# One matmul on block-diagonal operands, or two column tiles of 64: the sums and weighted sums of a windowed attention

## The chip, the cores and the metric

The kernel runs on one core of a Trainium2 chip. The metric is device time in microseconds (us) of that core, lower is better. TensorE (PE) does the matmuls, with a row of its own for loads of the stationary operand (PEld); VectorE (DVE), ScalarE (ACT) and GpSimd (POOL) do the elementwise work; SyncE (SP) issues most of the DMAs.

## The reference

Inputs are q, k and v of shape 8 x 8 x 576 x 64 (batch, heads, sequence, head dimension) and two weight matrices, 512 x 2048 and 2048 x 512.

```
scores = (q @ k.T) / sqrt(64)              # per batch and head, 576 x 576
scores = where(|i - j| <= 32, scores, -1e9)
attn   = exp(scores - max); attn = attn / (sum(attn) + 1e-9)
x      = attn @ v                          # 4608 tokens x 512 once the heads are joined
h      = x @ w_in; g = max(0.01 * h, h)
out    = g @ w_out                         # 4608 x 512, float32
```

The kernel needs no maximum, and it divides after the product with v: x = (sum of e * v) / (sum of e), with e the masked exponentials. So it has, per head, one sum of e over the keys and one weighted sum of v.

## The kernel before

**Tiling of the attention.** Two heads make a pair, four pairs a batch. One *step* is one pair and one half of the sequence (288 queries), so there are 64 steps: 8 batches x 2 halves x 4 pairs. The keys are cut into blocks of 64. The partitions of a step's tiles hold 64 keys of the first head (0 to 63) and 64 of the second (64 to 127).

The stationary operands are block-diagonal, 128 x 128: `kbd` holds a block of the transposed keys of the two heads, `vbd` a block of their values, and `ones_bd` two 64 x 64 blocks of ones; the other two quarters are zero. With such an operand one matmul works for both heads, and its output has the first head in partitions 0 to 63 and the second in 64 to 127.

**A step** has these parts:

- `score` (L275): five matmuls of `kbd` blocks with q into the PSUM tile `ps`, each for the 32 to 64 queries that see this block (in two interleaved columns, so 64 to 128 moving columns); then the exponential on ScalarE (L280) and the mask on GpSimd (L282), which gives `prob`. Blocks with even and odd numbers lie in two layers n of `prob`, so that every query has a place in each.
- `join` (L292, from step 12 on): VectorE adds the two layers into `both`.
- `sums` (L301, or L304 for the first 12 steps): one matmul of `ones_bd` with `both`, 288 moving columns, or two matmuls that accumulate over the two layers. The result `s` is inverted on VectorE (L309) into `r`.
- `product` (L320): five matmuls of `vbd` blocks with `prob`, with 64, 128, 96, 128 and 128 moving columns, together 544, that accumulate into `x`.
- `scaled` (L334): VectorE multiplies `x` by `r` into the ring `xT`, which the MLP reads.

**The MLP.** For each group of 288 tokens 16 tiles of h (L348, four matmuls of 288 columns each, 1024 in all) and then, for each 128 tokens, an output tile (L390, 16 matmuls of up to 512 columns, 592 in all). Before these, the activation is on ScalarE (L355).

**Order.** It is written out by hand: the engines get their instructions in the order of the program. The first 12 steps are laid out singly, with `sums` and `product` at separate places in part. From step 12 on, a plan gives every step a due time in PE time of the MLP, some 4 us apart, and `spend` calls `step` between two tiles. On TensorE a step of this stage is: five matmuls of `score` for the step after next, then `sums` (one matmul), then `product` (five matmuls), then the MLP again. Nothing in the plan's prices depends on the steps' own PE time.

**PSUM.** `s` and `x` have a buffer of 288 float32 columns each (one bank); `ps` has two banks and the MLP four.

Of the kernel before, what the change touches and what calls it, by code (L numbers as in the profile page):

```python
# [16 lines left out]
def kernel(  # L17
# [14 lines left out]
    nc = tc.nc  # L32
# [78 lines left out]
    ones_bd = const.tile([128, 128], BF16)  # L111
# [9 lines left out]
    vbd = [const.tile([128, NPAIR, NB, 128], BF16, name=f"vbd{i}") for i in range(2)]  # L121
# [145 lines left out]
    def where(i):  # L267
        return i // 8, (i // 4) % 2, i % 4
# [26 lines left out]
    def sums(i):  # L295

        b, hf, p = where(i)
        pr, both, _ = probs[i]
        s = xps.tile([128, HALF], FP32, name="s")
        if both is not None:  # L300
            nc.tensor.matmul(s, ones_bd, both, start=True, stop=True)  # L301
        else:
            for n in range(2):
                nc.tensor.matmul(  # L304
                    s, ones_bd, pr[:, n].rearrange("p c i -> p (c i)"),
                    start=(n == 0), stop=(n == 1),
                )
        r = recip.tile([128, HALF], FP32, name="r")
        nc.vector.reciprocal(r, s)  # L309
        probs[i][2] = r  # L310

    def product(i):

        b, hf, p = where(i)
        pr = probs[i][0]
        x = xps.tile([128, HALF], FP32, name="x")
        x_v = x.rearrange("p (c i) -> p c i", c=2)
        parts = [(n_, *block) for n_ in range(2) for block in WIN[hf][n_]]
        for n_, blk, i0, n in parts:
            nc.tensor.matmul(  # L320
                x_v[:, :, i0:i0 + n], vbd[b % 2][:, p, blk, :], pr[:, n_, :, i0:i0 + n],
                start=(blk == parts[0][1]), stop=(blk == parts[-1][1]), skip_group_check=True,
            )
        probs[i][1] = x

    def place(i):
# [9 lines left out]
    def weighted(i):  # L336
        if probs[i][2] is None:
            sums(i)
        product(i)
        scaled(i)  # L340
# [127 lines left out]
    cast_qk(0, 2, nc.vector)  # L468
    score(1)
    sums(0)  # L470
    next(first)
    next(first)
    product(0)
    keep_busy(ps, 0, 2)
    place_keys()
    cast_qk(0, 3, nc.scalar)
    load_w_in(0, 512)
    scaled(0)
    sums(1)
    keep_busy(ps, 0, 3)  # L480
    load_w_in(512, 1024)
# [10 lines left out]
    score(3)  # L492
    load_w_out(0)
    product(1)
    scaled(1)
    cast_v(0, 2, on_act=True)
# [150 lines left out]
```

## Time and profile before

| what | value |
|---|---|
| time, median of 2 runs | 319.7 us (319.49 and 319.91) |
| the profiled execution, first to last instruction | 318.5 us |
| PE busy | 303.2 us, 95%, 2449 matmuls |
| PEld busy | 204.3 us, 64%, 2449 loads |
| DVE busy | 218.2 us, 69% |
| POOL busy | 191.6 us, 60% |
| ACT busy | 182.6 us, 57% |
| granted TensorE clock, mean | 1.000 |
| matmuls of `sums` | 52 (L301) and 24 (L304) |
| matmuls of `product` | 320 (L320) |

The profiled execution is known by its span alone; the timed runs have what lies around it too, and their median is 1.2 us above the span. A row of the profile's groups gives the line, engine and operation, the output and the inputs with the tile names, the count, the busy time and the mean duration of one. Matmuls are pipelined: one starts before the one ahead has ended, so the recorded duration of one (286 ns for 288 columns) is longer than the time to the start of the next. Where a stream is dense the price of a matmul is that distance between starts, which the timeline gives. The share of a chain's line is the share of the span in which this line was what the end waited for.

### The profile page before, as it was taken

Reading aid. Unit: us, or ns where it says so; the run is one execution under the profiler, and the core shown is the slowest. Engines: PE = TensorE matmul, PEld = TensorE weight load, DVE = VectorE, ACT = ScalarE, POOL = GpSimd, SP = SyncE. Lnnn points to the kernel's source line nnn. Section 1 sums busy time; section 2 is a strip of 40 time slices with the busy share of each in tenths; the row PEclk is TensorE's granted clock in tenths of the full one; section 3 lists DMA queues with packets and bytes.
Section 4 is the critical chain, followed back from the end, with each engine's and each line's share of the span. In section 5 each row is a group of like instructions: output and inputs, shape, how many; then the busy total and the mean of one; then the engine's idle time right before and its main releaser. Section 6 shows DMA issues by size and latency. Waiting matters only on the chain.

```text
span 318.5 us, 6474 instructions
## 1 busy us (share of the span) xinstructions
PE 303.2 (95%) x2449; PEld 204.3 (64%) x2449; DVE 218.2 (69%) x259; ACT 182.6 (57%) x393; POOL 191.6 (60%) x251
## 2 busy tenths in 40 slices
PE   2679998999999999999999999999999999999996
PEld 1467774585765858576765858576665858576653
DVE  5678955869655997688755997688745988565100
ACT  7577698474652828374652828375552837464531
POOL 7798963974546866686546866586637866330000
PEclk9999999999999999999999999999999999999999
DMA  8999999997999995399735995399733430000101
GB/s 179 211 186 218 267 250 203 250 206 181 216 242 196 231 206 150 82 251 203 155 76 127 238 227 136 75 223 232 162 76 104 109 70 33 35 35 2 66 31 71
DMA packets 108400, 49.46 MB, mean 155 GB/s; under 512 B 68816, under 2 KB 103888, under 8 KB 108368
## 3 DMA queue, kind: packets, MB, share of 16 engines
q1 hardware_dynamic: 104144, 44.84, 66.8%
q0 software_dynamic: 4224, 4.19, 8.0%
q8 instruction: 19, 0.31, 0.4%
q14 instruction: 13, 0.11, 0.1%
HBM read 36.70 MB, written 9.44 MB: 145 GB/s over the span
## 4 chain that ended last, share of the span: by engine, by line
PE 89%; DMA 3%; DVE 2%; SPq 1%; POOL 1%; ACT 1%; issue 1%; DVEq 0%; ACTq 0%
PE mm L348 39%; PE mm L390 38%; PE x L320 5%; PE ps L275 4%; DMA kf<-in_k_dram 3%; PE s L301 2%; DVE r L309 2%; SPq L79 1%; POOL w_in_bf L448 1%; DVE xT L334 1%; PE tp L225 1%; PE s L304 1%; ACT vbd L203 0%; SPq L91 0%; POOL prob L282 0%
## 5 line engine op out<-in xcount | busy, mean ns | idle before, releaser
L309 DVE RECIPROCAL r<-s 128x288 f32<-128x288 f32 x64 | 125.2, 1956 | 56.5 <-PE s L301 53.3
L282 POOL TENSOR_TENSOR prob<-e,mask 128x576 bf16<-128x576 bf16 x64 | 81.5, 1274 | 87.8 <-ACT e L280 41.1
L348 PE MATMUL mm<-xT,w_in_bf 128*128 128x288 bf16 x1024 | 134.0, 286 | 0.3
L390 PE MATMUL mm<-w_out_bf,gT 128*128 128x512 bf16 (+2 forms) x592 | 130.4, 373 | 0.2 <-DMA w_out_bf<-in_moe_w_out_dram 0.2
L355 ACT ACTIVATE gT<-mm 128x288 bf16<-128x288 f32 x256 | 101.4, 412 | 24.8 <-PE mm L348 8.5
L348 PEld LDWEIGHTS <-w_in_bf 128*128 128x128 bf16 x1024 | 98.4, 98 | 24.8 <-issue 0.6
L390 PEld LDWEIGHTS <-gT 128*128 128x128 bf16 x592 | 56.3, 98 | 59.6 <-issue 0.3
L395 ACT ACTIVATE o_sb<-mm 128x512 f32<-128x512 f32 (+2 forms) x37 | 21.7, 586 | 92.0 <-PE mm L390 92.0
L280 ACT ACTIVATE e<-ps 128x576 bf16<-128x576 f32 x64 | 41.4, 648 | 9.4 <-PE ps L275 9.2
L197 POOL CAST kb<-kf 96x384 bf16<-96x384 f32 (+1 forms) x56 | 35.5, 656 | 4.6 <-DMA kf<-in_k_dram 4.6
L205 POOL CAST vbd<-vf 64x576 bf16<-64x576 f32 x50 | 34.5, 689 | 1.8 <-DMA vf<-in_v_dram 0.4
L334 DVE TENSOR_TENSOR xT<-x,r 128x288 bf16<-128x288 f32 x64 | 29.3, 458 | 8.2 <-PE x L320 1.2
L260 DVE COPY kbd<-kT 64x576 bf16<-64x576 bf16 x48 | 32.3, 672 | 0.3
L275 PE MATMUL ps<-qT,kbd 128*128 128x128 bf16 (+2 forms) x320 | 26.5, 215 | 1.8 <-DVE kbd L258 1.2
L275 PEld LDWEIGHTS <-kbd 128*128 128x128 bf16 x320 | 21.0, 100 | 10.6 <-DVE kbd L258 1.5
L320 PE MATMUL x<-prob,vbd 128*128 128x128 bf16 (+2 forms) x320 | 26.0, 213 | 1.3 <-ACT vbd L203 0.7
L197 POOL CAST qb<-qf 96x384 bf16<-96x384 f32 x48 | 24.5, 538 | 0.0
L320 PEld LDWEIGHTS <-vbd 128*128 128x128 bf16 x320 | 20.6, 99 | 3.9 <-ACT vbd L203 1.8
L292 DVE TENSOR_TENSOR both<-prob 128x288 bf16<-128x288 bf16 x52 | 19.7, 380 | 0.9
L301 PE MATMUL s<-both,ones_bd 128*128 128x288 bf16 x52 | 14.9, 286 | 0.0
L258 DVE COPY kbd<-kT 64x576 bf16<-64x576 bf16 x16 | 7.1, 444 | 8.7 <-ACT kT L239 8.6
L225 PE MATMUL tp<-ident,qb 96*128 96x96 bf16 x48 | 4.4, 243 | 6.2 <-DVE qb L197 6.2
(43 smaller groups left out, 86.6 us busy)
## 6 DMA issues: line engine op xcount, KB each, us to landing
qf<-in_q_dram SPq DMA_DIRECT2D x32, 288.0 KB, 4.5
kf<-in_k_dram SPq DMA_DIRECT2D x32, 288.0 KB, 5.0
vf<-in_v_dram SPq DMA_DIRECT2D x64, 144.0 KB, 4.2
out_dram<-o_sb SPq DMA_DIRECT2D x35, 256.0 KB, 3.6
w_in_bf<-in_moe_w_in_dram POOLq DMA_DIRECT2D x4, 512.0 KB, 8.6
w_out_bf<-in_moe_w_out_dram POOLq DMA_DIRECT2D x4, 512.0 KB, 16.8
qT<-qb SPq DMA_TRANSPOSE x24, 4.1
kT<-kb SPq DMA_TRANSPOSE x24, 3.2
```

What stands on the lines that cost most here:

```text
L197: eng.tensor_copy(out=to, in_=tok)
L205: nc.gpsimd.tensor_copy(out=vbd[b % 2][r, p, :, r], in_=vf[b, p][r])
L260: nc.vector.tensor_copy(out=to.rearrange("p n (m c) -> p n c m", c=2), in_=kT[r].rearrange("p (c n m) -> p n c m", c=2, n=NB),)
L275: nc.tensor.matmul(ps_v[:, n_, :, i0:i0 + n], kbd[b % 2][:, p, blk], by_c[:, :, hf * EVEN + i0:hf * EVEN + i0 + n], start=True, stop=True,)
L280: nc.scalar.activation(out=e, in_=ps[:, P0:P0 + 2 * HALF], func=AF.Exp, scale=scale)
L282: nc.gpsimd.tensor_mul(pr.rearrange("p n c i -> p (n c i)"), e, mask[hf].rearrange("p n c i -> p (n c i)"),)
L309: nc.vector.reciprocal(r, s)
L320: nc.tensor.matmul(x_v[:, :, i0:i0 + n], vbd[b % 2][:, p, blk, :], pr[:, n_, :, i0:i0 + n], start=(blk == parts[0][1]), stop=(blk == parts ...
L334: nc.vector.tensor_mul(place(i), x, r)
L348: nc.tensor.matmul(h[:, 0:HALF], w_in_bf[:, c, ts(f, 128)], xT[:, c, ds(g * HALF % RING, HALF)], start=(c == 0), stop=(c == DMC - 1),)
L355: nc.scalar.activation(out=gT[:, f, ds(g * HALF % RING, HALF)].rearrange("p (i c) -> p i c", c=2), in_=h[:, 0:HALF].rearrange("p (c i) -> ...
L390: nc.tensor.matmul(o[:, lo:hi], gT[:, f, ds(128 * j % RING, 128)], w_out_bf[:, f, lo:hi], start=(f == 0), stop=(f == FFC - 1),)
```

## The change

`sums` and `product` call TensorE once for each head of the pair. The stationary operand of a call is a half of the columns of the same tile, 64 of 128, with all 128 partitions (so with the half that is zero); the moving operand is the same as before; the output is the half of the PSUM tile that belongs to this head, partitions 0 to 63 or 64 to 127. Every matmul of these two functions, and its load of the stationary operand, becomes two. The two halves of a pair stand directly behind each other. `score`, the MLP, the tiles, buffers and the order are unchanged.

```diff
@@ sums
         s = xps.tile([128, HALF], FP32, name="s")
-        if both is not None:
-            nc.tensor.matmul(s, ones_bd, both, start=True, stop=True)
-        else:
-            for n in range(2):
+        for n in range(1 if both is not None else 2):
+            cols = both if both is not None else pr[:, n].rearrange("p c i -> p (c i)")
+            for r in (slice(0, 64), slice(64, 128)):
                 nc.tensor.matmul(
-                    s, ones_bd, pr[:, n].rearrange("p c i -> p (c i)"),
-                    start=(n == 0), stop=(n == 1),
+                    s[r], ones_bd[:, r], cols, skip_group_check=True,
+                    start=(n == 0), stop=(both is not None or n == 1),
                 )
@@ product
         for n_, blk, i0, n in parts:
-            nc.tensor.matmul(
-                x_v[:, :, i0:i0 + n], vbd[b % 2][:, p, blk, :], pr[:, n_, :, i0:i0 + n],
-                start=(blk == parts[0][1]), stop=(blk == parts[-1][1]), skip_group_check=True,
-            )
+            for r in (slice(0, 64), slice(64, 128)):
+                nc.tensor.matmul(
+                    x_v[r, :, i0:i0 + n], vbd[b % 2][:, p, blk, r], pr[:, n_, :, i0:i0 + n],
+                    start=(blk == parts[0][1]), stop=(blk == parts[-1][1]), skip_group_check=True,
+                )
```

## The prediction

> **What bounds the kernel now.** I read the page's busy times first, then the chain that ended last, then windows by stage, and last the timeline of TensorE around one step. From the page, the busy times, the slices (PE's busy tenths and granted clock) and the chain:
>
> ```profile
> PE 303.2 (95%) x2449; PEld 204.3 (64%) x2449; DVE 218.2 (69%) x259; ACT 182.6 (57%) x393; POOL 191.6 (60%) x251
> ...
> PE   2679998999999999999999999999999999999996
> ...
> PEclk9999999999999999999999999999999999999999
> ...
> PE 89%; DMA 3%; DVE 2%; SPq 1%; POOL 1%; ACT 1%; issue 1%; DVEq 0%; ACTq 0%
> ```
>
> PE is the bound from the fourth slice on, at the full clock, and the chain is PE for 89% of the span. The windows by stage (span, then PE and PEld busy with counts, the other engines, clock, DMA) say where that is exact:
>
> ```profile
> 0.00:36.00 36.00, 24.96 (x236) 19.22 (x237) 27.34 (x34) 25.36 (x44) 31.11 (x44) 1.00 1.12 207
> 36.00:61.00 25.00, 23.80 (x215) 15.61 (x214) 16.51 (x22) 20.66 (x41) 17.02 (x19) 1.00 1.15 235
> 61.00:290.00 229.00, 229.00 (x1838) 154.36 (x1837) 170.29 (x202) 126.73 (x287) 143.49 (x190) 1.00 0.73 152
> ```
>
> From 61 to 290 us PE has no idle time at all, while DVE, ACT and POOL have 59 us or more each. A microsecond added to PE there is a microsecond of the kernel; one taken from another engine is worth nothing. In the first 36 us PE idles for 11.0 us, and it waits for VectorE and GpSimd.
>
> One step of the dense stage, in the timeline of PE (start, busy time, line, count):
>
> ```profile
> 199.91 0.29 PE L301 MATMUL s<-both,ones_bd 128*128 128x288 bf16 x1
> 200.03 0.40 PE L320 MATMUL x<-prob,vbd 128*128 128x96 bf16 x5
> 200.27 0.65 PE L348 MATMUL mm<-xT,w_in_bf 128*128 128x288 bf16 x4
> ```
>
> By starts, `sums` holds PE for 200.03 - 199.91 = 0.12 us and `product` for 200.27 - 200.03 = 0.24 us: 0.36 us a step. Five loads ran beside those five matmuls and cost nothing visible.
>
> **What the change removes and adds.** It removes no work that PE pays for. A matmul is paid by its moving columns (544 columns in 0.24 us, 288 in 0.12 us), and both halves stream the same columns as the whole did. It adds one matmul and one load for each there was: 320 + 52 + 24 = 396 of each. The exponential, mask, reciprocal and scaling are the same instructions. No DMA is added or moved. No wait is added either: `s` and `x` are still handed on when the last of their matmuls is done. There are three terms, each unknown in this trace, since every matmul in it uses all 128 columns.
>
> *Term 1, the second half's stream.* If the array takes the two halves side by side, the term is 0. If it takes them one after the other, every step of `sums` and `product` is paid twice. That is 52 x 0.36 = 18.7 us for the later steps. In the first 12, `sums` is two matmuls (0.24 us), so 12 x 0.48 = 5.8 us. Together 24.5 us. Between these ends no row decides; I take 0, because the halves use different columns of the array and different output partitions, and keep 24.5 us for the range. *TensorEngine Tiling (Array Packing)* of the Trainium skill, section Key Properties, has tiles work independently and in parallel; no run here shows it.
>
> *Term 2, going from the whole array to half tiles and back.* A step goes whole (`score`), half (`sums`, `product`), whole (MLP). For the 52 later steps that is one stretch of half tiles each. For the first 12 I counted the stretches in the timeline: 8 where a `sums` stands beside a `product` and 8 single ones, 16 in all. 68 stretches have 136 borders. The lower end of a border's price is 0, if the array lets the next form flow in behind the last; less than nothing is excluded, since PE's slots are already as short as their columns. The upper end is a pipeline that must run empty. How long that is can be read from the groups:
>
> ```profile
> L348 PE MATMUL mm<-xT,w_in_bf 128*128 128x288 bf16 x1024 | 134.0, 286 | 0.3
> ...
> L320 PEld LDWEIGHTS <-vbd 128*128 128x128 bf16 x320 | 20.6, 99 | 3.9 <-ACT vbd L203 1.8
> ...
> L301 PE MATMUL s<-both,ones_bd 128*128 128x288 bf16 x52 | 14.9, 286 | 0.0
> ```
>
> and from the chain in order of time:
>
> ```profile
> 102.68 3.43 PE mm L348 x28
> ...
> 111.72 3.45 PE mm L390 x16
> ```
>
> 28 matmuls of 288 columns take 3.43 us, 0.1225 us each, but one is recorded as 0.286: 0.164 us is its tail, hidden by the next one. With 512 columns it is the same, 0.379 (the mean of this form) - 3.45/16 = 0.163. If the next matmul may not enter before the tail is out, a border costs 0.164 us, and 136 x 0.164 = 22.3 us. A load that couldn't be brought forward over the border adds up to its recorded 0.098 us, 13.3 us for all of them. I take the full tail and no load, because the tail is the only thing in these rows that a change of form must have to wait for, and a load may come ahead of its matmul's slot as it does everywhere else in the trace. In the first 36 us, 12 of the stretches (24 borders, 3.9 us) lie in a stage with idle PE; there the chain runs s, reciprocal, scaling, x, so most of their price still reaches the end, and if all of it were covered the term would be 18.4 us.
>
> The Trainium skill speaks against the change here. *TensorEngine Tiling (Array Packing)*, Key Properties, says that a change of tiling mode, unlike a change of tile within one, drains the TensorE. No run here shows such a change; with the rule term 2 is the upper end above, and without it the sum would be zero.
>
> *Term 3, the loads.* There are 10 in a product instead of 5, and 2 in a sum instead of 1. At the lower end they hide beside the matmuls like the 320 in the row above. At the upper end each of the 396 added ones shows with its 0.098 us, 38.8 us. I take 0: before, five loads of 0.10 us were issued within the product's 0.24 us without opening a gap. Half of the upper end, 19.4 us, is a rival below.
>
> A second rule against it: the same page, Gotcha 2, excludes Fast Weight Load under column tiling, and *TensorE: Matmul & The Clock Gate*, LDWEIGHTS, gives an ordinary load its columns divided by 1.2 in nanoseconds, 53 ns for 64. By that, an estimate, ten loads one behind the other need 0.53 us where the product had 0.24, and 64 products would add 18.8 us to my sum; in this trace loads start as little as 0.03 us apart.
>
> **The sum.** 0 + 22.3 + 0 on the profiled execution's 318.5 us gives a span of 340.8. The median of the runs is 1.2 us above the span, so 342.0 us, 7.0% above 319.7. Where PE takes longer, what else is late? VectorE waits for `sums` anyway (53.3 us idle before the reciprocal, all behind L301), and its 170.3 us of work in 229 have room. The steps come some 4 us apart and their chain on VectorE is 1.96 + 0.46 us, so `xT` gets later with PE itself and not beyond it.
>
> **Rivals.**
>
> *Nothing to pay (not slower).* The halves run side by side and a border costs no more than the ordinary distance between matmuls. The point that decides is the border's price: 2% is 6.4 us, and 6.4 / 136 = 0.047 us, under a third of the tail. It needs an array in which the halves' streams follow the whole ones down the pipeline. For it speaks that only the column side is split and that all 128 rows still sum downwards; against it, that the tail is nowhere in the trace crossed by a change of form. Price 0 to 6 us, about 321 us.
>
> *Halves in turn, borders free.* The instructions are built, but the array takes the second half after the first, so that the change doesn't do what it says. Term 1 alone: 319.7 + 24.5 = 344 us. It can't be told from my forecast by the time alone, only by the starts.
>
> *Halves in turn and borders dear.* 24.5 + 22.3 = 46.8 us: 366 us.
>
> *Loads that show.* Halves side by side, borders at the tail, half of the loads' upper end: 22.3 + 19.4 = 41.7 us, 361 us. For it: `product` has slots as short as 0.03 us, and twice the loads for them. Against it: PEld is busy only 64% of the span.
>
> *Faster.* There is no slot to shorten: from 61 us on PE is full and its slots are the moving columns, which are the same. I know of no mechanism.
>
> **How the numbers follow.** Forecast (342, its own range 336 to 348) 0.42; halves in turn with free borders 0.13; loads that show 0.16; halves in turn and dear borders 0.12; nothing to pay 0.10; all upper ends together (370 and more) 0.05; faster 0.02. The likeliest is 342.0. The range reaches from 323 (most of the free case left out, 0.08) to 369 (0.05 left out above, 0.02 faster below). By the 2% that a measurement of this kernel can tell from no change: faster 0.02, same 0.10, slower 0.88.
>
> **What would show it.** In the changed kernel's profile L301 and L320's groups should count 104 and 640 (line numbers aside), with 64 columns. If term 1 is right, the two halves start within a few hundredths of a microsecond of each other, and `product` takes about 0.24 us; if it takes 0.48, they run in turn. If term 2 is right, the last MLP or score matmul and the first half tile start about 0.16 us further apart than their columns need, and so do the last half tile and the next whole matmul, with PE's busy share perhaps unchanged, since the tail counts as busy. If term 3 is wrong, the distances between matmuls inside `product` grow to those of its loads. The span from 61 to 290 us should grow by about 52 x 0.33 = 17 us. I would be wrong if the array orders the halves otherwise, or if a border costs much less or more than the recorded tail, which is modelled by the profiler and not seen.

## Result and profile after

The changed kernel takes 333.26 us (333.13 and 333.40) against 319.70 before: 1.0425 times as long, 95% interval 1.0395 to 1.0455. The span of the profiled execution went from 318.5 to 331.7 us, 13.2 more. The page's lines on busy times, chain and the two functions, of the changed kernel:

```profile
PE 315.5 (95%) x2825; PEld 205.8 (62%) x2845; DVE 221.7 (67%) x259; ACT 182.7 (55%) x393; POOL 192.2 (58%) x251
...
PE mm L348 38%; PE mm L390 37%; PE s L303 5%; PE x L320 5%; PE ps L275 4%; DMA kf<-in_k_dram 2%; PE tp L225 1%; DVE qb L197 1%; POOL prob L282 1%; ACT vbd L203 1%; ACT e L280 1%; ACT kT L239 0%; SPq L79 0%; PE ps L402 0%; ACT qT L233 0%
...
L320 PE MATMUL x<-prob,vbd 128*64 128x128 bf16 (+2 forms) x640 | 27.0, 214 | 1.0 <-ACT vbd L203 1.0
...
L320 PEld LDWEIGHTS <-vbd 128*64 128x64 bf16 x640 | 22.5, 111 | 3.5 <-ACT vbd L203 1.4
...
L303 PE MATMUL s<-both,ones_bd 128*64 128x288 bf16 x104 | 16.3, 310 | 0.0
```

The forms are now 128*64 (rows by columns of the array), 640 and 104 of them (and 48 in the `sums` of the first 12 steps), and 396 loads were added (2845 against 2449). Of the 2845 matmuls 20 of L390 have no record in this trace. The row of `product` before:

```profile
L320 PE MATMUL x<-prob,vbd 128*128 128x128 bf16 (+2 forms) x320 | 26.0, 213 | 1.3 <-ACT vbd L203 0.7
```

The busy time of `product` rose by only 1.0 us (26.0 to 27.0) for twice the matmuls: busy time is the union of the records, and the halves lie over each other. PE's share is 95% as before. So the groups alone don't show where 13 us went. The share of `sums` in the chain rose from 3% (L301 and L304) to 5%; that of `score` and `product` stayed. One step of the dense stage, in the timeline of PE:

```profile
216.88 0.40 PE L275 MATMUL ps<-qT,kbd 128*128 128x64 bf16 x5
217.21 0.31 PE L303 MATMUL s<-both,ones_bd 128*64 128x288 bf16 x2
217.36 0.41 PE L320 MATMUL x<-prob,vbd 128*64 128x64 bf16 x10
217.70 3.48 PE L348 MATMUL mm<-xT,w_in_bf 128*128 128x288 bf16 x27
```

By starts, `score` now holds PE for 0.33 us (0.24 before), `sums` for 0.15 (0.12) and `product` for 0.34 (0.24). With the window of the timeline narrowed, the last `score` and the last `product` of a step stand alone, before (the step at 199.91 that the prediction shows) and after:

```profile
199.85 0.22 PE L275 MATMUL ps<-qT,kbd 128*128 128x128 bf16 x1
...
200.22 0.22 PE L320 MATMUL x<-prob,vbd 128*128 128x128 bf16 x1
```

```profile
217.06 0.22 PE L275 MATMUL ps<-qT,kbd 128*128 128x128 bf16 x1
...
217.54 0.22 PE L320 MATMUL x<-prob,vbd 128*64 128x128 bf16 x2
```

From the last `score` to `sums` there were 0.06 us (199.85 to 199.91) and are now 0.15 (217.06 to 217.21); from the last `product` to the MLP there were 0.05 (200.22 to 200.27) and are now 0.16 (217.54 to 217.70). The starts of the single records of this step say what each part is, in nanoseconds (nearly all of the other steps from 66 us on agree within 3 ns):

| part of a dense step | before | after | more |
|---|---|---|---|
| second half behind the first | - | 2 to 4 | |
| last `score` start to first `sums` start (128 columns, 56 ordinary) | 56 | 149 | 93 |
| first `sums` start to first `product` start | 122 | 147 | 25 |
| first to last block of `product` | 183 | 189 | 6 |
| last `product` start to first MLP start | 56 | 152 to 155 | 96 |
| first MLP matmul to the second (288 columns, 122 ordinary) | 122 | 132 | 10 |
| sum | | | 230 |

The halves run side by side. What is paid is the passage between the whole array and the half tiles, once into them and once out, and behind each passage a little more for the first matmul. From the first `sums` of step 12 to the last matmul the kernel before takes 249.3 us and the changed one 261.1, which is 11.8 more; 52 x 0.230 = 12.0 us account for it. The other 1.4 us come before step 12.

### The profile page after: what moved, and what is told of

Read it like the earlier page. It is cut to its first block, busy times and chain, and to the rows that moved or that the text cites. A ratio compares the mean times of both kernels' runs of the same rounds, so it can differ in the third digit from the quotient of the medians.

```text
span 331.7 us, 7246 instructions
## 1 busy us (share of the span) xinstructions
PE 315.5 (95%) x2825; PEld 205.8 (62%) x2845; DVE 221.7 (67%) x259; ACT 182.7 (55%) x393; POOL 192.2 (58%) x251
## 4 chain that ended last, share of the span: by engine, by line
PE 91%; ACT 2%; DMA 2%; issue 1%; DVE 1%; POOL 1%; SPq 0%; ACTq 0%; POOLq 0%; DVEq 0%
PE mm L348 38%; PE mm L390 37%; PE s L303 5%; PE x L320 5%; PE ps L275 4%; DMA kf<-in_k_dram 2%; PE tp L225 1%; DVE qb L197 1%; POOL prob L282 1%; ACT vbd L203 1%; ACT e L280 1%; ACT kT L239 0%; SPq L79 0%; PE ps L402 0%; ACT qT L233 0%
## 5 line engine op out<-in xcount | busy, mean ns | idle before, releaser
L390 PE MATMUL mm<-w_out_bf,gT 128*128 128x512 bf16 (+2 forms) x572 | 128.9, 373 | 1.5 <-issue 0.6
L348 PEld LDWEIGHTS <-w_in_bf 128*128 128x128 bf16 x1024 | 96.6, 98 | 28.6 <-issue 1.2
L390 PEld LDWEIGHTS <-gT 128*128 128x128 bf16 x592 | 55.5, 98 | 61.2
L205 POOL CAST vbd<-vf 64x576 bf16<-64x576 f32 x50 | 35.6, 712 | 1.5
L260 DVE COPY kbd<-kT 64x576 bf16<-64x576 bf16 x48 | 32.3, 674 | 0.3
L320 PE MATMUL x<-prob,vbd 128*64 128x128 bf16 (+2 forms) x640 | 27.0, 214 | 1.0 <-ACT vbd L203 1.0
L320 PEld LDWEIGHTS <-vbd 128*64 128x64 bf16 x640 | 22.5, 111 | 3.5 <-ACT vbd L203 1.4
L197 POOL CAST qb<-qf 96x384 bf16<-96x384 f32 x48 | 22.9, 503 | 0.0
L292 DVE TENSOR_TENSOR both<-prob 128x288 bf16<-128x288 bf16 x52 | 20.4, 392 | 0.7
L303 PE MATMUL s<-both,ones_bd 128*64 128x288 bf16 x104 | 16.3, 310 | 0.0
L303 PEld LDWEIGHTS <-ones_bd 128*64 128x64 bf16 x152 | 7.8, 108 | 8.0 <-issue 1.8
```

The lines of the kernel that those rows point to most:

```text
L197: eng.tensor_copy(out=to, in_=tok)
L205: nc.gpsimd.tensor_copy(out=vbd[b % 2][r, p, :, r], in_=vf[b, p][r])
L260: nc.vector.tensor_copy(out=to.rearrange("p n (m c) -> p n c m", c=2), in_=kT[r].rearrange("p (c n m) -> p n c m", c=2, n=NB),)
L303: nc.tensor.matmul(s[r], ones_bd[:, r], cols, skip_group_check=True, start=(n == 0), stop=(both is not None or n == 1),)
L320: nc.tensor.matmul(x_v[r, :, i0:i0 + n], vbd[b % 2][:, p, blk, r], pr[:, n_, :, i0:i0 + n], start=(blk == parts[0][1]), stop=(blk == parts ...
L348: nc.tensor.matmul(h[:, 0:HALF], w_in_bf[:, c, ts(f, 128)], xT[:, c, ds(g * HALF % RING, HALF)], start=(c == 0), stop=(c == DMC - 1),)
```

## Experiments

**Theories.** *Border*: the price belongs to each change of form (a *border*, between the whole array and half tiles), some 0.22 us for a stretch of half tiles, and the number of half matmuls doesn't matter. *Per matmul*: the price belongs to the 396 added matmuls or their loads, 13.2/396 = 0.033 us each. The table above was read from one trace; the experiments change the number of borders and of matmuls independently.

**One part alone.** The sums in halves and the products whole (the diff is against the changed kernel):

```diff
-            for r in (slice(0, 64), slice(64, 128)):
-                nc.tensor.matmul(x_v[r, :, i0:i0 + n], vbd[b % 2][:, p, blk, r], ...)
+            nc.tensor.matmul(x_v[:, :, i0:i0 + n], vbd[b % 2][:, p, blk, :], ...)
```

> Only the sums are split; the products are whole matmuls as before. Border theory (each change of form between whole array and half tiles costs about 0.1 us, 0.22 us for a stretch of half tiles): 64 stretches remain of 68, so nearly the whole loss stays: 331 to 333 us, and a dense step gains 0.22 us over the kernel before. Rival, the price comes with each added matmul and load of 64 columns (13.2 us / 396 = 0.033 us): 76 of the 396 remain, +2.5 us: 322 us.

Measured: 334.29 us, ratio to the kernel before 1.0457 (1.0432 to 1.0481), 1 us above the range and 12 above the rival's time. With 76 of the 396 added matmuls the whole loss is there. Its timeline of PE in a dense step:

```profile
132.35 0.40 PE L275 MATMUL ps<-qT,kbd 128*128 128x64 bf16 x5
132.68 0.31 PE L303 MATMUL s<-both,ones_bd 128*64 128x288 bf16 x2
132.93 0.41 PE L319 MATMUL x<-prob,vbd 128*128 128x96 bf16 x5
133.18 0.65 PE L347 MATMUL mm<-xT,w_in_bf 128*128 128x288 bf16 x4
```

The way out of the half tiles now stands between `sums` and `product` (0.25 us from start to start, against 0.15), and `product` to MLP is back at 0.25. The border moved with the edit.

The products in halves and the sums whole (the diff is against the kernel before):

```diff
-            nc.tensor.matmul(x_v[:, :, i0:i0 + n], vbd[b % 2][:, p, blk, :], ...)
+            for r in (slice(0, 64), slice(64, 128)):
+                nc.tensor.matmul(x_v[r, :, i0:i0 + n], vbd[b % 2][:, p, blk, r], ...)
```

> Only the products are split; the sums are whole. Border theory: again 64 stretches, 331 to 333 us, so that the two parts alone lose together about twice what they lose in one. Rival, price by the added matmul: 320 of 396, +10.6 us, 330 us, and the two parts add up to the whole change.

Measured: 332.77 us, 1.0416 (1.0388 to 1.0443), inside the range and 2.8 us above the rival's time. Alone the parts lose 14.4 and 12.9 us, 27.3 together, against 13.6 in one: the two share their borders, and these are nearly all that they cost.

**More half matmuls, no more borders in the dense stage.** The scores in halves too:

```diff
-                nc.tensor.matmul(
-                    ps_v[:, n_, :, i0:i0 + n], kbd[b % 2][:, p, blk],
+                for r in (slice(0, 64), slice(64, 128)):
+                    nc.tensor.matmul(
+                        ps_v[r, n_, :, i0:i0 + n], kbd[b % 2][:, p, blk, r],
```

> The score matmuls are split too: 320 more matmuls and loads, but in the dense stage they stand directly ahead of the sums, so the borders there stay two a step. Border theory: 333 to 336 us (a dense step unchanged within 0.02 us; some more stretches among the first 12 steps). Rival, price by the added matmul: +10.6 us on the changed kernel, 344 us.

Measured: 334.68 us, 1.0473 (1.0439 to 1.0508): inside the border theory's range, 9 us under the rival's. The timeline of PE shows the border ahead of `score` now, 0.31 us after the start of a matmul of 512 columns that is 0.215 long elsewhere, and `sums` at 0.12 us as in the kernel before, since its first load no longer stands behind a border:

```profile
141.65 0.38 PE L391 MATMUL mm<-w_out_bf,gT 128*128 128x512 bf16 x1
141.96 0.43 PE L276 MATMUL ps<-qT,kbd 128*64 128x64 bf16 x10
142.22 0.29 PE L304 MATMUL s<-both,ones_bd 128*64 128x288 bf16 x2
142.34 0.41 PE L321 MATMUL x<-prob,vbd 128*64 128x64 bf16 x10
142.69 0.79 PE L349 MATMUL mm<-xT,w_in_bf 128*128 128x288 bf16 x5
```

**Fewer half matmuls, three times the borders.** Whole and half blocks in turn inside a product:

```diff
-        for n_, blk, i0, n in parts:
-            for r in (slice(0, 64), slice(64, 128)):
+        for at_, (n_, blk, i0, n) in enumerate(parts):
+            for r in (slice(0, 128),) if at_ % 2 else (slice(0, 64), slice(64, 128)):
```

> As the changed kernel, but the second and fourth of the five blocks of a product are whole matmuls, so a step has three stretches of half tiles instead of one. Border theory: two more stretches of 0.22 us in each of 64 steps, +28 us on 333: 361 us. Rival, price by the added matmul: 128 fewer half pairs, 4 us less: 329 us.

Measured: 362.88 us, 1.1352 (1.1321 to 1.1383), where the rival had 329.

```profile
154.18 0.40 PE L275 MATMUL ps<-qT,kbd 128*128 128x64 bf16 x5
154.52 0.31 PE L303 MATMUL s<-both,ones_bd 128*64 128x288 bf16 x2
154.66 0.86 PE L320 MATMUL x<-prob,vbd 128*64 128x64 bf16 x8
155.46 0.66 PE L348 MATMUL mm<-xT,w_in_bf 128*128 128x288 bf16 x4
```

This timeline has `product` at 0.80 us from start to start, with eight matmuls; five whole ones took 0.24 and ten halves 0.34. By the single records, the way from the last `score` to the MLP is 1.089 us in this kernel and 0.417 before: 0.672 more, three times 0.224. (The expectation counted 28 us on top of the changed kernel; 29.6 came.)

**Almost no borders, six times the added matmuls.** Everything but the transposes in halves, the MLP too:

```diff
-                h[:, 0:HALF], w_in_bf[:, c, ts(f, 128)], xT[:, c, ...],
+            for r in (0, 64): ...
+                h[r:r + 64, 0:HALF], w_in_bf[:, c, ds(128 * f + r, 64)], xT[:, c, ...],
...
-                    o[:, lo:hi], gT[:, f, ds(128 * j % RING, 128)], w_out_bf[:, f, lo:hi],
+                for r in (0, 64): ...
+                    o[r:r + 64, lo:hi], gT[:, f, ds(128 * j % RING + r, 64)], w_out_bf[:, f, lo:hi],
```

> Every matmul but the transposes is split into two halves: sums, products, scores, both MLP matmuls and the fillers, about 2350 added matmuls and loads. The borders are gone except round the transposes of the first 50 us. Border theory: 320 to 324 us, close to the kernel before although it has six times the added matmuls of the change. Rival, price by the added matmul or load (0.033 us): +78 us, 398 us.

Measured: 321.77 us, 1.0066 (1.0043 to 1.0089), where a price by the matmul gives 398. The page's busy line and one step:

```profile
PE 304.9 (95%) x4802; PEld 255.5 (80%) x4802; DVE 221.6 (69%) x259; ACT 182.8 (57%) x393; POOL 191.7 (60%) x251
```

```profile
137.03 0.43 PE L276 MATMUL ps<-qT,kbd 128*64 128x64 bf16 x10
137.28 0.32 PE L304 MATMUL s<-both,ones_bd 128*64 128x288 bf16 x2
137.40 0.43 PE L321 MATMUL x<-prob,vbd 128*64 128x64 bf16 x10
137.64 0.69 PE L350 MATMUL mm<-xT,w_in_bf 128*64 128x288 bf16 x8
```

With 4802 matmuls instead of 2449 the step has the slots of the kernel before (0.12 and 0.24 us; from `score` to the MLP 0.606 us against 0.601). Half tiles cost next to nothing so long as TensorE stays in them. Cut by the starts of the h matmuls into sixteenths of their count, the way from the seventh to the last takes 160.4 us (137.6 to 298.0), before 160.2 (136.8 to 297.0). Of the 1.0 us that the span is longer, 0.7 are there at the third sixteenth (64.9 us against 64.2); in that stage the whole-array transposes of the second batch stand between half tiles four times. The single records have the borders there too: the first transpose starts 96 ns later than the columns ahead of it need (in one of the four still later), the first half tile behind the transposes 94 ns later (136 ns where the kernel before has 42). With the loads behind them that is about 0.22 us each time, 0.9 us for the four; from the second to the third sixteenth this kernel loses 1.0 us.

**Other tiles, the same borders.** Four tiles of 32 columns in place of two of 64 in `sums` and `product`:

```diff
-            for r in (slice(0, 64), slice(64, 128)):
+            for r in (slice(0, 32), slice(32, 64), slice(64, 96), slice(96, 128)):
```

> Sums and products in four tiles of 32 columns instead of two of 64, 1188 added matmuls and loads instead of 396, the same 136 borders. Border theory: 331 to 335 us; the load that shows behind the border into the tiles is of 32 columns, so it may be 0.013 us shorter a step. Rival, price by the added matmul: +39 us on 320, 359 us.

Measured: 332.73 us, 1.0414 (1.0384 to 1.0445). Twice the matmuls of the changed kernel in these functions, and no more time. The passages are the same (by the records, 93 ns more on the way in and 96 on the way out). One thing differs, and it tells what the 25 ns behind the border are. The lines of `sums` and `product` in a step:

```profile
140.60 0.31 PE L303 MATMUL s<-both,ones_bd 128*32 128x288 bf16 x4
140.73 0.41 PE L320 MATMUL x<-prob,vbd 128*32 128x64 bf16 x20
```

By the records, `sums` takes 133 ns to the first `product`, against 147 with tiles of 64 and 122 within a form. The excess is 11 to 12 ns for 32 columns and 25 for 64, so by these two points it goes with the columns loaded. Behind a border the first load of the new form shows, because it isn't brought forward over the border: before, the load of `sums` starts 54 ns ahead of its matmul (199.856 and 199.910 us), in the changed kernel 2 ns ahead (217.210 and 217.212). Back into the whole array the load has 128 columns and shows with only 10 ns, so one price for a column doesn't fit both ways.

**Can half tiles gain?** If borders are all they cost, and a kernel wholly in half tiles has nearly none, the two tiles can be given different moving columns. For one head tile 0 takes an even key block and tile 1 an odd one, so the layers lie on partitions and the two heads along the free axis. Then `sums` and `product` contract over 128 keys instead of 64 keys and 64 zeros, with 288 columns each in every step (parts of the diff against the kernel before):

```diff
@@ score
+        for a in range(2): ...   # head a, the blocks of the two layers n_ in turn
+            ps_v[64 * n_:64 * n_ + 64, a, :, i0:i0 + n], kbd[b % 2][:, p, blk, 64 * a:64 * a + 64], ...
@@ sums
+            s[r], ones_bd[:, r], pr[:, a].rearrange("p c i -> p (c i)"), start=True, stop=True,
@@ product
+        cuts = ((0, 48, 80, 112, 144), (0, 32, 64, 96, 144))[hf]
+            x_v[r, :, lo:hi], vbd[b % 2][:, p, 4 * hf + at_ + 1, r], pr[:, a, :, lo:hi],
```

> Everything but the transposes in half tiles, and the two tiles of a pair now take different moving columns. Scores: tile 0 takes an even key block, tile 1 an odd one, for one head after the other, so that the partitions of the exponentials hold the two layers of keys and the free axis the two heads. Sums and products: tile 0 takes the first head, tile 1 the second, each contracting over 128 keys instead of 64 keys and 64 zeros; four pairs of 288 columns instead of five of 544, one sum of 288 columns in every step, and no joining of the layers on VectorE. The values are stored for each of the eight pairs of neighbouring blocks, which makes each cast on GpSimd about 1.8 times as long. If tiles with different moving data run side by side: 0.12 us less a step than with all halves, 64 x 0.12 = 7.5 us: 314 us, faster than the kernel before. Rival, tiles side by side only with the same moving columns: scores, sums and products in turn, 0.45 + 0.24 + 0.24 us a step instead of 0.60, 21 us more than with all halves: 343 us. Rival, GpSimd's longer casts (some 50 us more on 192 us) get into the chain of the exponentials: between 318 and 330 us with gaps of TensorE behind them.

Measured: 331.41 us, 1.0361 (1.0337 to 1.0385). Against the expectation it is slower, and above the rival of the casts (318 to 330) too. It isn't for want of overlap: the way from the seventh sixteenth of the h matmuls to the last takes 157.5 us, before 160.2. Its chain of waits runs by the values' loads and casts before 66 us and leaves TensorE from 111.6 to 137.6 us, by the mask and the casts on GpSimd, the transposes of the keys and VectorE. Behind the gaps the matmuls were slower as well: the granted clock was 0.66 from 120 to 125 us and 0.86 from 130 to 140, and 1.00 in the kernel before. So the next kernels lighten the loads and casts (against this kernel; the second differs from the first only by what the comment says):

```diff
-            for a in range(2):
-                nc.sync.dma_start(out=t[64 * n_:64 * n_ + 64, 0:cnt, a], in_=by_blk[:, a, n_::2])
+        for a in range(2):
+            nc.sync.dma_start(out=t[:, 0:4, a], in_=v[b, 2 * p + a, 0:512].rearrange("(c p) d -> p c d", p=128))
+        nc.sync.dma_start(out=t[0:64, 4], in_=v[b, 2 * p:2 * p + 2, 512:576].rearrange("a q d -> q a d"))
...
+        nc.vector.tensor_copy(out=to[:, :, 0], in_=tok[:, 0:4])      # ScalarE for the first eight pairs in the second kernel
```

> As the kernel with the two layers in the two tiles, but without what is seen to stall it there (from 105 to 134 us the chain runs by the exponential, the mask, the casts of q, k and v on GpSimd, the transposes of the keys and VectorE, for some 10 us; in the first 66 us by the loads and casts of the values): the values come by three DMAs a pair instead of four, and are cast by one operation of 128 x 512 on VectorE, in place of the joining that went, and two of 64 x 512 on GpSimd (ScalarE for the first eight pairs). If those stalls were all that hid the shorter steps: 314 to 317 us, faster than the kernel before by 1 to 2%. Rival, the halves with different moving columns themselves are slower in the dense stage: 325 us and more, with TensorE full and its steps no shorter than before.

> The same, but with all three casts of the first eight pairs on ScalarE, so that VectorE gets none of them in the opening stage. If VectorE is what the opening waits for, 1 to 3 us faster than with the cast on VectorE; if ScalarE is, as much slower. 313 to 320 us either way.

Measured: 322.99 us, 1.0107 (1.0081 to 1.0134), and 322.03 us, 1.0090 (1.0058 to 1.0122). Both lie above what was expected of them (314 to 317 and 313 to 320), and the 1 us between them is within the spread of their runs. Of the second, the timeline of PE in a step:

```profile
177.54 0.45 PE L284 MATMUL ps<-qT,kbd 128*64 128x128 bf16 x9
177.77 0.29 PE L313 MATMUL s<-prob,ones_bd 128*64 128x288 bf16 x1
177.83 0.21 PE L284 MATMUL ps<-qT,kbd 128*64 128x96 bf16 x1
177.87 0.29 PE L313 MATMUL s<-prob,ones_bd 128*64 128x288 bf16 x1
177.89 0.36 PE L331 MATMUL x<-prob,vbd 128*64 128x64 bf16 x7
178.06 0.29 PE L360 MATMUL mm<-xT,w_in_bf 128*64 128x288 bf16 x1
```

The tiles run side by side with different data, and even in different functions: a `sums` of one tile starts (177.77) ahead of the last `score` of the other (177.83). From the start of `score` to that of the MLP most steps from 83 us on take 0.506 to 0.520 us, before 0.601: about 0.09 us less, where 0.12 was expected. From the seventh sixteenth of the h matmuls (141.0 us, before 136.8) to the last (298.3, before 297.0) this kernel takes 157.3 us and the one before 160.2. These 3 us are lost again earlier: 1.2 us between 35 and 66 us (about 0.9 of them at the borders round the four groups of transposes here too), and 3.6 between 103 and 141, where the chain in order of time (start, duration, line) leaves TensorE:

```profile
106.48 1.14 POOL kb L197 x2
107.62 5.00 DMA kT<-kb
112.64 1.29 DVE kbd L266
113.97 0.74 DVE kbd L266
114.74 1.97 DVE r L318
```

VectorE waits for a transpose of keys and is late with the reciprocals of three steps. Two kernels move this. One places the keys a step later, with the same edit to the kernel before as its control:

```diff
-        landing.append((8 * (b - 1) + 4 + p, b, p, kT))
+        landing.append((8 * (b - 1) + 5 + p, b, p, kT))
```

> As the kernel before it in this series (two layers in the two tiles, casts of the first eight pairs on ScalarE), but VectorE places the transposed keys one step later. In the trace of that one TensorE loses 4 to 5 us from 107 to 128 us, where VectorE waits for the transposes of the keys (the chain runs by that DMA and VectorE); from 141 us on its sixteen tiles of h and what goes with them are 3.0 us shorter over 160 us than before. If the late keys were the cause: 316 to 318.5 us, 0.3 to 1% faster than the kernel before. Rival, the stall moves to another wait: 321 us or more.

> The kernel before with the keys placed one step later and nothing else: it shows no such stall, so nothing is expected of it, 319 to 321 us. If it is faster too, the last gain isn't due to the tiles.

Measured: 321.03 us, 1.0052 (1.0038 to 1.0067), and the control 322.76 us, 1.0100 (1.0086 to 1.0114). The stall went: the stage from the fifth to the seventh sixteenth takes 34.4 us, with the keys where they were 37.9, before 34.3. But the first matmul of h starts 1.0 us later (24.6 us against 23.6), and the way from the seventh sixteenth to the last takes 158.8 us instead of 157.3, so the time is the rival's, above the 316 to 318.5 that were expected. The expectation of the control was wrong: a later place of the keys costs the kernel before 1%. Its trace shows seven new waits of `score` for the placed keys (L260), 2.0 us of the 2.9 us that its span is longer. Against its own control the kernel with different columns in the tiles is 1.7 us faster, by the two medians of one chip, but the control had been slowed by the edit; against the kernel before it is 1.5 us slower. The other casts q and k a step earlier:

```diff
-            qk_due.setdefault(8 * (b - 1) + p + (1 if b == 2 else 2), []).append((b, p))
+            qk_due.setdefault(8 * (b - 1) + p + 1, []).append((b, p))
```

> As the kernel with two layers in the two tiles and the first casts on ScalarE, with the keys placed where they were; instead the casts of q and k on GpSimd, and with them the transposes, come one step earlier from the fourth batch on (the third has them there already). Placing the keys a step later made the kernel before 1.0% slower, so that lever had a price of its own. If the late transposes cause the stall of 107 to 128 us, it goes, and the 3.0 us that the dense stage gains remain, against 1 to 2 us lost in the first 66 us: 317 to 318.5 us, 0.3 to 0.8% faster than the kernel before. Rival, the earlier casts push the masks of the exponentials back on GpSimd and the stall stays: 321 us or more.

Measured: 322.77 us, 1.0109 (1.0088 to 1.0131). The stall stayed for the most part: the stage from the fifth to the seventh sixteenth takes 36.4 us. The rival is right in its outcome; that the casts push the masks back was not shown. That the stall goes when the keys are placed later, and shrinks only from 37.9 to 36.4 us when they are cast earlier, fits the chain, in which VectorE is held up by the wait for the keys. Whether they have a place that costs nothing elsewhere stays open. None of these kernels beats the kernel before.

## Why the prediction was right, and which term was mis-sized

- *What bounds the kernel*: TensorE, full from 61 us on, so that every microsecond added there shows. Right: the 52 later steps account for 11.8 of the 13.2 us.
- *Term 1, the second half's stream, taken at 0*: right. The halves start 2 to 4 ns apart, and with everything in halves the step's slots are the old ones. The rivals with halves in turn (344 and 366 us) fall, and so does the one with nothing to pay (321 us): it needed borders under 0.047 us, and a border with its load costs 0.11 to 0.12. *TensorEngine Tiling (Array Packing)* of the Trainium skill, Key Properties, agrees: tiles work independently.
- *Term 2, the borders, 136 x 0.164 = 22.3 us*: right in what is paid for, the changes of form, and the mis-sized term. The upper end, a pipeline that must run empty, was read from the recorded duration beyond the slot, 0.164 us. That end is modelled, as the prediction itself warned. The start of the next matmul shows 0.093 us on the way in and 0.096 on the way out, 0.19 us for a stretch instead of 0.33. The page's rule that a change of tiling mode drains the TensorE, in the same section, gives no figure; a gap at each change of form is what it leads one to expect. The trace shows the gap and not what runs empty in it. In every run here the form of the load changes together with the form of the matmul, so whether the array or the path of the loads has to run empty is not shown.
- *The load at a border, taken at 0 of an upper end of 0.098 us*: wrong by a little. The first load of the new form shows with 25 ns into tiles of 64 columns and 10 ns back into the whole array, 0.035 us for a stretch.
- *Term 3, the loads within a stretch, taken at 0*: right. Ten loads of 64 columns make `product` 6 ns longer, and the rival of loads that show (361 us) falls. The same page's Gotcha 2 excludes Fast Weight Load here, and the trace bears that out in form (the load's operand is one run of 64 elements now, four of 32 before); but the estimate of 18.8 us from *TensorE: Matmul & The Clock Gate*, LDWEIGHTS, doesn't show: loads of 64 columns went by at two per slot of 28 ns.
- *The first 36 us*: by 16 stretches at 0.23 us, 3.7 us were due before step 12, and 1.4 us came. Of the 12 stretches in the first 36 us, where PE idles, almost nothing is left: the second sixteenth of the h matmuls starts 0.2 us later (35.3 us against 35.1). The prediction let most of it reach the end.
- *The sum*: 342.0 us forecast, 333.3 measured, +7.0% against +4.25%. The measured time lies below the 336 to 348 of the forecast's own case; the direction and what is paid for were right, the size (22.3 us against 13.6) was 1.6 times too large. Of the 9.1 us of span that were too much, 5.2 belong to the 52 later steps and 3.9 to the first 12. Had the borders been priced at 0.115 us (half of 0.23) instead of 0.164, 52 later steps would give 12.0 us and the forecast 332 to 335.

## What to carry to other kernels

Count the changes of tile form, not the matmuls: here a stretch of column tiles between whole-array matmuls cost 0.22 to 0.23 us of TensorE whatever was in it, from 2 matmuls to 24. Column tiles that streamed the same columns as the whole array had nothing to win here and paid for the borders. Where the two tiles took different columns a step became shorter (by about 0.09 us of 0.60), with the whole neighbourhood in tiles; no kernel here turned that into a shorter time than that of the kernel before, and each lost the gain again in other stages. A busy share is blind to such a price: PE stood at 95% before and after, and only the distance between the starts of matmuls showed it.

## What was unexpected about the hardware

- The passage between forms is shorter than the recorded tail of a matmul: 93 to 96 ns against 164.
- In the first 19 us of the kernel before (16 in the changed one) TensorE runs at half pace by its starts (a filler of 224 columns every 187 ns, later every 96), though the granted clock reads 1.00 there. That 1.00 is no measurement: the first record of the clock in that trace begins at 19.15 us. In the changed kernel the passages take 130 to 140 ns in that stretch, about 1.4 times as long as later and not twice.
- Column tiles follow each other independently across functions: with different columns in the tiles, a `sums` starts 59 ns ahead of a `score` that stands ahead of it in the program (177.768 and 177.827 us).
- Placing the transposed keys one step (4 us) later costs the kernel before 3.2 us, though TensorE waited for nothing in its dense stage: seven times a `score` waits for them then, 2.0 us in all.
